# A three-operation kernel: converted weights stored from the source's tile, doubled conversion steps spread out, and a third of batch 0's factors loaded early into a tile of its own

## The chip, the cores and the metric

The kernel runs on one core of a Trainium2 chip. The metric is the device time of one execution in microseconds (us), as the median of several runs. The engines are named as in the profile: PE is TensorE (matmul), PEld its weight load, DVE is VectorE, ACT is ScalarE, POOL is GpSimd, and SP is the Sync engine, which here only issues transfers.

## The reference

Input `x` is 8 batches of 3072 positions by 256 channels. Three operations follow each other:

```python
X = np.fft.rfft(x, axis=1)
Yr = Xr @ w_r - Xi @ w_i + b_r ; Yi = Xr @ w_i + Xi @ w_r + b_i
Y  = sign(Y) * max(|Y| - 0.01, 0)          # on both parts
x  = irfft(Y, n=3072)                      # 24576 x 256 tokens
# soft mixture of 8 experts with 4 slots each
logits = x @ phi
d = softmax of logits over the tokens ; slots = d.T @ x
slots = relu(slots @ w1) @ w2              # per expert
c = softmax of logits over the 32 slots ; x = c @ slots
# feed-forward layer
h = x @ w_in                               # 256 -> 2048
out = (h * tanh(softplus(h))) @ w_out
```

`w_in` and `w_out` arrive as 64-bit floats, given to the kernel as pairs of 32-bit integers, so the kernel has to convert them to 32-bit floats itself.

## The kernel before, in words

The work falls into three stages. In the first, of about 610 us, the 8 batches are transformed, thresholded and transformed back, the logits and both softmaxes are formed, and the slots are summed up over all tokens. In the second, of about 25 us, the experts work on the 32 slots. In the third, of about 1210 us, the feed-forward layer runs over 48 blocks of 512 tokens, each in 8 steps, so 384 steps.

In the first stage the order of everything is written out by hand. `at(pos, fn, ...)` puts a piece of work at a position, the pieces are sorted by position and then issued one after the other, so each engine and each queue gets its own instructions in that order. The unit of the position is a step `k`: there are 4 steps to a batch, 32 in all, and each runs the linear part (`linear`, lines 306 to 331) for a quarter of the batch's frequencies. Around step `k` stand the second transform stage (`stage2`, lines 268 to 283), about one step ahead of the linear part that uses it, the loads of its input (`load_b`, line 255, tile `bt`, at k - 1.91, so for a step that comes later), the first stage of later batches (`load_x`, line 225, `stage1`, lines 238 and 241, `store_a`, line 248), and the softmax chain of the batch before (`sturn` to `ctrans`, lines 374 to 466), which repeats every four steps. `ctrans` writes the combination factors `c` of batch b to the DRAM tensor `c_d[b]`, once as rounded values and once as remainders; for batch 0 it does so at position 7.24.

In `linear` VectorE adds `p` (line 319), ScalarE makes `cl` and the other threshold from it (lines 326 and 327), and POOL subtracts the two into `yt` (line 328). `cl` has one buffer. All of these are in order on their engines with the conversions below.

The conversions (`conv`, lines 571 to 605) turn a piece of 128 x 256 weights into floats in seven small pieces of work: step 0 loads the integers into the tile `cvs` (line 578, on the Sync queue, two buffers); step 1 is a product on POOL into `cvc` (line 588, one buffer); steps 2 to 5 are four operations and a scaling on VectorE (lines 590 to 597) that use `cva`, `cvs` and `cvc`; step 6 is a sum on POOL (line 600 for `w_in`, line 604 for `w_out`). For `w_in` the sum is written over `cvc` and stored from there to the DRAM tensor `win_d`, by a transfer that POOL issues (line 601). For `w_out` the sum is written over the source's tile, and pieces of it are split later (`cut`, `sums`). There are 16 pieces of `w_in` and then 16 of `w_out`. Their places are the list `homes`: piece i has its VectorE work at `homes[i]`, its load 0.6 ahead of that and its first POOL operation 0.21 ahead. Every step from 4 to 29 has a piece at k - 0.13, and six steps, 5, 7, 8, 10, 11 and 13, have a second one at k - 0.7.

Between the stages the loads for the third are issued on the Sync queue: two expert weights `raw` (line 853), `win` (line 778, from `win_d`), and the weight pairs `wc` and `whl` of the eight steps (`load_w`, line 772), and among them the factors `ctt` of batch 0 from `c_d[0]`, in two halves of four transfers of 192 KB each (`c_fetch`, line 810), the first half right behind the first weight pair, the second behind the third.

The third stage (`ffn`) starts with `prep`, which multiplies the expert outputs with `win` (line 949), splits the result, spreads it (line 959) and copies it to `mst` (lines 964 and 966). Step p then makes two `h` matmuls from `mst` and `ctt` (line 974), ScalarE gates them (line 990) into `g` or `u`, both engines split the results (lines 996 to 1020), and some steps later `omm` multiplies them with the weights into `oa` to `od` (lines 1033 and 1044). A block reads 8 of the 24 columns of `ctt`: blocks 0 and 1 of a batch the first 8, blocks 2 and 3 the next 8, blocks 4 and 5 the last. The first twelve-matmul step of `omm` is placed behind the `h` of step 3.

Of the kernel before, what the change touches and what calls it, by code (L numbers as in the profile page):

```python
# [8 lines left out]
F32 = mybir.dt.float32  # L9
# [4 lines left out]
ALU = mybir.AluOpType  # L14
# [56 lines left out]
def body(ctx, tc, x, w_r, w_i, b_r, b_i, phi, w1, w2, w_in, w_out, cbig, ct, out, dbg=None, stop=False):  # L71
# [5 lines left out]
    def at(pos, fn, *a):  # L77
        items.append((round(pos, 4), len(items), fn, a))
# [4 lines left out]
    cb = keep.tile([128, 128 * 3 + 32], F32, name="cb")  # L83
    f1, f1t, ident, sel = cb[:, 0:128], cb[:, 128:256], cb[:, 256:384], cb[:, 384:416]
    sit = keep.tile([128, 2, NS], F32, name="sit")
    win_d = dram.tile([D, FF], F32, name="win_d")
    wn_d = dram.tile([4, 128, 2, 2 * D], F32, name="wn_d")
    wf_d = dram.tile([4, 128, 2, 7 * 128], F32, name="wf_d")
# [485 lines left out]
    def conv(srcd, dstd, i, step):  # L574
        n, v, p = CW, nc.vector, nc.gpsimd
        if step == 0:
            cv["n", i] = late[1].tile([128, n, 2], I32, tag="cs", bufs=2, name="cvs")
            nc.sync.dma_start(out=cv["n", i], in_=srcd[i])
            return
        if step == 1:  # L580
            src = cv["src"] = cv.pop(("n", i))
            cv.update(lo=src[:, :, 0].bitcast(U32), hi=src[:, :, 1])
            for t in "ac":
                cv[t] = late[1].tile([128, n], I32, tag="c" + t, name="cv" + t)
        lo, hi, a, c = (cv[t] for t in ("lo", "hi", "a", "c"))
        if step == 1:
            hf = hi.bitcast(F32)
            p.tensor_tensor(c.bitcast(F32), hf, hf, op=ALU.mult)
        elif step == 2:
            v.tensor_scalar(a, hi, 5, 2, op0=ALU.logical_shift_left, op1=ALU.logical_shift_right)  # L590
            v.scalar_tensor_tensor(a, hi, -0x40000000, a, op0=ALU.bitwise_and, op1=ALU.bitwise_or)
        elif step == 3:
            v.scalar_tensor_tensor(a.bitcast(F32), c.bitcast(F32), TINY2, a.bitcast(F32), op0=ALU.is_ge, op1=ALU.mult)
        elif step == 4:
            v.tensor_scalar(hi, a, -0x800000, None, op0=ALU.bitwise_and)
        elif step == 5:
            v.scalar_tensor_tensor(c.bitcast(F32), lo, 2.0 ** -52, hi.bitcast(F32), op0=ALU.mult, op1=ALU.mult)
        else:
            if dstd is not None:
                p.tensor_tensor(c.bitcast(F32), a.bitcast(F32), c.bitcast(F32), op=ALU.add)  # L600
                p.dma_start(out=dstd[i], in_=c.bitcast(F32))
                return
            o = cv["src"].rearrange("p n t -> p (n t)").bitcast(F32)
            p.tensor_tensor(o[:, 0:n].rearrange("p (e a c) -> p a e c", e=2, a=4), a.bitcast(F32).rearrange("p (a e c) -> p a e c", e=2, a=4),
                            c.bitcast(F32).rearrange("p (a e c) -> p a e c", e=2, a=4), op=ALU.add)
            cv["o", i] = o
# [38 lines left out]

    SIDE = {b: [4 * b + z for z in (-5.825, -4.825, -4.525, -3.825, -2.825, -2.525)] for b in range(3, NB - 1)}

    at(-9, setup)
    at(-5.5, fill, 22)
    at(-5.2, weights)  # L650
    for c in range(4):
# [49 lines left out]
    si, di = view(w_in, win_d)  # L701
    so, do = [w_out.bitcast(I32).rearrange("(q p t) c -> q t p c", q=4, t=4)[i // 4][i % 4].rearrange("p (f t) -> p f t", t=2) for i in range(16)], None
    ncv = len(si) + len(so)
    homes = sorted([k - 0.13 for k in range(4, 30)] + [k - 0.7 for k in (5, 7, 8, 10, 11, 13)])
    assert len(homes) == ncv
    for i in range(ncv):
        s_, d_, ii = (si, di, i) if i < len(si) else (so, do, i - len(si))
# [26 lines left out]
    with tc.manual_schedule():  # L734
        for _, _, fn, a in sorted(items, key=lambda v: v[:2]):
            fn(*a)
        if dbg is not None:
            nc.sync.dma_start(out=dbg["m_all"], in_=m_run[(NB + 1) % 2])
            nc.sync.dma_start(out=dbg["ds_all"], in_=d_acc)
            nc.sync.dma_start(out=dbg["s_all"], in_=s_acc)  # L740
            nc.sync.dma_start(out=dbg["c0"], in_=c_d[0])
            nc.sync.dma_start(out=dbg["wout"], in_=wout_d)
            nc.sync.dma_start(out=dbg["win"], in_=win_d)

        left.close()
        if stop:
            ex.close()
            ctx_r.close()
            return

        big = ctx.enter_context(tc.tile_pool(name="big", bufs=1))
        win = big.tile([128, 16, D], F32, name="win")
        sot = big.tile([128, 2, NS], F32, name="sot")
        rep = big.tile([128, 2, 4, NS], F32R, name="rep")
        mstp = ctx.enter_context(tc.tile_pool(name="mstp", bufs=1))
        hsp = ctx.enter_context(tc.tile_pool(name="hsp", bufs=1))
        ctp = [ctx.enter_context(tc.tile_pool(name="ctp0", bufs=1))]
        ct_t = {}
        ht = mstp.tile([128, 2, 8, 128], F32, tag="mst", name="ht")
        hs = [hsp.tile([128, FE], F32, name="hs"), big.tile([128, FE], F32, tag="wof", bufs=2, name="hs")]  # L760
        w_t = {}

        def load_w(p, pool=None):
            if p in FAST:
                t = big.tile([128, 2048], F32R, tag="whl", bufs=4, name="whl")[:, 0:1792]
                src = wf_d[p // 2].rearrange("p r f -> p (r f)")
                w_t[p] = t.rearrange("p (r k m) -> p r k m", r=2, k=7)
            else:
                t = (big if pool is None else pool).tile([128, 4 * D], F32R, tag="wof" if pool is None else "wc%d" % p, bufs=2 if pool is None else 1, name="wc")
                src = wn_d[p // 2].rearrange("p r f -> p (r f)")  # L770
                w_t[p] = t.rearrange("p (r i e m) -> p r i e m", r=2, i=2, e=2)
            nc.sync.dma_start(out=t.bitcast(F32), in_=src)

        def load_rest(ex):
            for i in range(2):
                ex.load(2, 6 + i, None, big.tile([128, 8, D], F32, tag="whl", bufs=4, name="raw"))
            for h in range(2):
                nc.sync.dma_start(out=win[:, 8 * h:8 * h + 8].rearrange("p t d -> p (t d)"), in_=win_d[128 * h:128 * h + 128])
            load_w(0)
            c_fetch(tc, ctp, ct_t, c_d, 0, (0, 2))  # L780
            load_w(1)
            for i in range(2):
                for r in range(2):
                    s2 = sel[:, None, :].to_broadcast([128, 2, NS])
                    if i == r:
                        nc.vector.tensor_copy(rep[:, i, 2 * r:2 * r + 2], s2)
                    else:
                        nc.vector.tensor_scalar(rep[:, i, 2 * r:2 * r + 2], s2, 0.0, None, op0=ALU.mult)

        ex.run(hs, ht, psum, sit, ident, sot, load_rest)  # L790
        load_w(2)
        c_fetch(tc, ctp, ct_t, c_d, 0, (2, 4))
        load_w(3)
        ex.close()
        ctx_r.close()
        pst.close()
        psh = ctx.enter_context(tc.tile_pool(name="psh", bufs=2, space=PSUM))
        pso = ctx.enter_context(tc.tile_pool(name="pso", bufs=2, space=PSUM))
        mst = mstp.tile([128, FF], F32R, tag="mst", name="mst")
        ctp.append(ctx.enter_context(tc.tile_pool(name="ctp1", bufs=1)))  # L800
        ffn(ctx, tc, NB, mst, w_t, win, c_d, out.rearrange("(b p n) d -> b p n d", b=NB, n=N2), ctp, ct_t, psh, pso, sot, rep, load_w)


def c_fetch(tc, ctp, ct_t, c_d, b, js=(0, 4)):

    if js[0] == 0:
        ct_t[b] = ctp[b % 2].tile([128, N2, 128], F32R, tag="ct", name="ctt")
    n = slice(6 * js[0], 6 * js[1])
    for r in range(4):
        tc.nc.sync.dma_start(out=ct_t[b][32 * r:32 * r + 32, n].bitcast(F32).rearrange("s (j i) t -> s j (i t)", i=6),  # L810
                             in_=c_d[b][r % 2][js[0]:js[1]].rearrange("j s i t -> s j (i t)"))
# [109 lines left out]
FAST = (1, 3, 5, 7)  # L921


def ffn(ctx, tc, NB, mst, w_t, win, c_d, out, ctp, ct_t, psh, pso, sot, rep, load_w):

    nc = tc.nc
    gp = ctx.enter_context(tc.tile_pool(name="gp", bufs=2))
# [5 lines left out]
    h_t, s_t, acc = {}, {}, {}  # L933
    for p in range(4, 8):
        load_w(p, pmp)
    zero = pmp.tile([128, 256], F32, name="zero")
    nc.gpsimd.memset(zero, 0.0)

# [29 lines left out]
    def hidden(p):  # L968
        blk, c = divmod(p, NPR)
        b, m = divmod(blk, NB4)  # L970
        h_t[p] = [psh.tile([128, 512], F32, tag="h", name="h") for _ in range(2)]
        for i in range(2):
            f = 2 * c + i
            nc.tensor.matmul(h_t[p][i].rearrange("p (n t) -> p n t", n=8), lhsT=mst[:, f * 128:f * 128 + 128],  # L974
                             rhs=ct_t[b][:, 8 * (m // 2):8 * (m // 2) + 8, 64 * (m % 2):64 * (m % 2) + 64], start=True, stop=True)

    def gate(p):
        h = h_t.pop(p)
# [145 lines left out]
```

## Time and profile before

| | us |
|---|---|
| median of 3 runs | 1854.81 |
| lowest and highest of them | 1852.15, 1858.98 |
| profiled execution, its own time | 1850.49 |
| its span, first to last instruction | 1848.1 |
| PE busy | 1803.0 |
| DVE busy | 1506.6 |
| ACT busy | 1380.0 |
| POOL busy | 264.8 |

A busy share over the whole span mixes three stages with different limits, so it only says which engine to look at. A row of the timeline gives the start of an instruction, how long it took, its engine, its line in the kernel, what it writes and reads, and in brackets how long the engine stood still ahead of it and what ended that. The granted clock is a share of TensorE's full speed; 0.50 is the lower of its two levels, 1.2 GHz.

### The profile page before, as it was taken

To read this page: it belongs to the slowest core of one execution; us is meant where nothing else is said; L and a number is where in the kernel's file an instruction comes from. 1 tells how busy PE (TensorE), PEld (TensorE's weight loads), DVE (VectorE), ACT (ScalarE), POOL (GpSimd) and SP (SyncE) were. 2 spreads that over 40 slices of the span, in tenths; PEclk is the share of its full clock that TensorE was granted. 3 is DMA by queue.
4 is the path that set the end of the run, shared out by engine and by line. 5 is a ranking of instruction groups with operands and counts; after the bars stand their busy time and mean duration, and the time that the engine had idled before them with its cause. 6 is when DMAs were issued, how large, how long until landed. Compare 5 with 4: busy or idle time off the path is not lost.

```text
span 1848.1 us, 32080 instructions
## 1 busy us (share of the span) xinstructions
PE 1803.0 (98%) x12438; PEld 1547.6 (84%) x12438; DVE 1506.6 (82%) x2158; ACT 1380.0 (75%) x2237; POOL 264.8 (14%) x342
## 2 busy tenths in 40 slices
PE   7999999999998899999999999999999999999998
PEld 5777778887887488888888888888888888888887
DVE  5366867666667489999999999999999999999997
ACT  4665767767765388888888888888888888888885
POOL 0233433544542000000000000000000000000000
PEclk8999999999999999999999999999999999999999
DMA  7776756666654930020020011002002002000001
GB/s 177 181 183 171 185 154 172 185 181 166 165 156 179 341 106 24 24 54 16 24 58 24 23 34 43 17 24 58 24 23 58 19 17 58 24 23 24 24 19 29
DMA packets 174663, 159.99 MB, mean 87 GB/s; under 512 B 111392, under 2 KB 143776, under 8 KB 172592
## 3 DMA queue, kind: packets, MB, share of 16 engines
q1 hardware_dynamic: 166848, 147.16, 30.2%
q0 software_dynamic: 2656, 7.90, 1.3%
q10 hardware_dynamic: 5008, 2.88, 0.7%
q8 instruction: 98, 1.61, 0.4%
q14 instruction: 53, 0.43, 0.1%
HBM read 96.55 MB, written 61.34 MB: 85 GB/s over the span
## 4 chain that ended last, share of the span: by engine, by line
PE 86%; DVE 4%; issue 3%; ACT 3%; DMA 3%; POOL 2%; SPq 0%; POOLq 0%; DVEq 0%; ACTq 0%
PE oa L1033 14%; PE ob L1033 14%; PE h L974 10%; PE l L306 8%; PE oa L1044 7%; PE oc L1044 7%; PE od L1044 7%; PE s L268 4%; PE ob L1044 4%; PE s L238 2%; PE tr L361 2%; PE pp L339 1%; POOL yt L328 1%; PE sps L529 1%; DMA ctt<-c_d 1%
## 5 line engine op out<-in xcount | busy, mean ns | idle before, releaser
L1018 DVE TENSOR_TENSOR sl<-u,sh 128x1792 fp32r<-128x1792 f32 x192 | 387.7, 2019 | 1.1 <-ACT sh L1013 1.1
L990 ACT ACTIVATE g<-h 128x512 f32<-128x512 f32 x384 | 208.8, 595 | 149.0 <-PE h L974 145.2
L1020 DVE TENSOR_TENSOR gl<-g,gh 128x1024 fp32r<-128x1024 f32 x191 | 231.7, 1213 | 83.6 <-ACT gh L1001 83.6
L974 PE MATMUL h<-ctt,mst 128*128 128x512 f32 x768 | 242.4, 397 | 4.6 <-DMA ctt<-c_d 3.1
L1033 PE MATMUL oa<-gh,wc 128*128 128x512 f32 x768 | 238.9, 392 | 0.0
L1033 PE MATMUL ob<-gh,wc 128*128 128x512 f32 x768 | 236.8, 390 | 0.0
L1013 ACT ACTIVATE sh<-u 128x1024 fp32r<-128x1024 f32 x192 | 201.4, 1049 | 45.3 <-DVE u L1008 45.3
L990 ACT ACTIVATE u<-h 128x512 f32<-128x512 f32 x384 | 207.6, 593 | 9.5 <-PE h L974 0.4
L1001 ACT ACTIVATE gh<-g 128x1024 fp32r<-128x1024 f32 x191 | 202.9, 1062 | 6.1
L984 POOL TENSOR_TENSOR sh<-zero 128x256 fp32r<-128x256 f32 x48 | 37.8, 788 | 1137.6 <-PE ob L1044 1137.5
L326 ACT ACTIVATE cl<-p,tup 128x384 f32<-128x384 f32 x124 | 76.3, 616 | 143.2 <-DVE p L319 90.2
L1033 PEld LDWEIGHTS oa<-gh,wc 128*128 128x128 f32 x768 | 144.7, 189 | 34.0
L1033 PEld LDWEIGHTS ob<-gh,wc 128*128 128x128 f32 x768 | 144.5, 188 | 30.1
L999 ACT ACTIVATE sh<-u 128x768 fp32r<-128x768 f32 x192 | 162.7, 847 | 9.0
L328 POOL TENSOR_TENSOR yt<-cl,p 128x384 f32<-128x384 f32 x124 | 126.4, 1019 | 261.0 <-ACT p L327 168.2
L974 PEld LDWEIGHTS h<-ctt,mst 128*128 128x128 f32 x768 | 132.8, 191 | 22.7 <-ACT g L990 3.6
L1006 DVE TENSOR_TENSOR u<-u 128x512 f32<-128x512 f32 x192 | 150.6, 784 | 0.0
L1033 PE MATMUL oa<-gl,wc 128*128 128x512 f32 x384 | 150.4, 392 | 0.0
L1033 PE MATMUL ob<-gl,wc 128*128 128x512 f32 x384 | 149.4, 389 | 0.0
L1044 PE MATMUL od<-sh,whl 128*128 128x256 f32 x720 | 147.7, 281 | 0.0
L1044 PE MATMUL oa<-sh,whl 128*128 128x256 f32 x768 | 146.1, 283 | 0.0
L1044 PE MATMUL oc<-sh,whl 128*128 128x256 f32 x720 | 140.5, 283 | 0.0
(236 smaller groups left out, 3948.9 us busy)
## 6 DMA issues: line engine op xcount, KB each, us to landing
out_dram<-ot SPq DMA_DIRECT2D x380, 64.0 KB, 1.8
xc<-in_x_dram SPq DMA_DIRECT2D x84, 256.0 KB, 4.7
sdr<-a SPq DMA_DIRECT2D x84, 256.0 KB, 4.1
bt<-sdr SPq DMA_DIRECT2D x84, 256.0 KB, 5.6
ctt<-c_d SPq DMA_DIRECT2D x28, 384.0 KB, 6.8
w1t<-in_moe_w_dram SPq DMA_DIRECT2D x6, 1024.0 KB, 6.9
c_d<-chl SPq DMA_DIRECT2D x14, 384.0 KB, 3.0
w2t<-in_moe_w_dram SPq DMA_DIRECT2D x5, 1024.0 KB, 11.1
```

What stands on the lines that cost most here:

```text
L306: nc.tensor.matmul(full[:, 0:48 * nq].rearrange("p (q f) -> p q f", f=48), lhsT=ww[:, h, es], rhs=spec(xx, h), start=n == 0, stop=n == 5)
L328: nc.gpsimd.tensor_sub(o, cl, p)
L974: nc.tensor.matmul(h_t[p][i].rearrange("p (n t) -> p n t", n=8), lhsT=mst[:, f * 128:f * 128 + 128], rhs=ct_t[b][:, 8 * (m // 2):8 * (m // ...
L990: nc.scalar.activation(out=v[i], in_=h[i], func=AF.Mish)
L999: nc.scalar.activation(out=gh[:, 0:3], in_=g[:, 1:4], func=AF.Copy)
L1001: nc.scalar.activation(out=gh, in_=g, func=AF.Copy)
L1006: nc.vector.tensor_sub(g[:, 4:6], g[:, 0:1].to_broadcast([128, 2, 256]), g[:, 1:3])
L1013: nc.scalar.activation(out=gh[:, 3:7], in_=g[:, 4:8], func=AF.Copy)
L1018: nc.vector.tensor_sub(gl, g[:, 1:8], gh[:, 0:7].bitcast(F32))
L1020: nc.vector.tensor_sub(gl, g, gh.bitcast(F32))
L1033: nc.tensor.matmul(ps, lhsT=w[:, r, i, e], rhs=x[:, i], start=c == 0 and i == 0 and n == 0, stop=p == NQ - 2 and i == 1 and n == 2)
L1044: nc.tensor.matmul(ps[:, half], lhsT=w[:, r, k], rhs=y[:, x], start=False, stop=c == FAST[-1] and n == 2 and ((t, half) in (("c", 1), ("d" ...
```

## The change

There are three edits. First, the sum of a converted piece of `w_in` is written over the source's tile `cvs`, as that of `w_out` is already, and stored to `win_d` from there. Second, the six steps with two conversions are 6, 8, 10, 12, 14 and 16 in place of 5, 7, 8, 10, 11 and 13. Third, a tile `c0` of its own holds the first 8 columns of batch 0's factors; it is loaded at position 12.05 of the first stage by eight transfers on the Sync queue, and blocks 0 and 1 read it. The two half loads of `ctt` for batch 0 between the stages go; one whole load of four transfers is issued in `ffn` behind the last weight load.

```diff
--- before.py
+++ after.py
@@ -83,6 +83,7 @@
     cb = keep.tile([128, 128 * 3 + 32], F32, name="cb")
     f1, f1t, ident, sel = cb[:, 0:128], cb[:, 128:256], cb[:, 256:384], cb[:, 384:416]
     sit = keep.tile([128, 2, NS], F32, name="sit")
+    c0 = keep.tile([128, 8, 128], F32R, name="c0")
     win_d = dram.tile([D, FF], F32, name="win_d")
     wn_d = dram.tile([4, 128, 2, 2 * D], F32, name="wn_d")
     wf_d = dram.tile([4, 128, 2, 7 * 128], F32, name="wf_d")
@@ -596,11 +597,11 @@
         elif step == 5:
             v.scalar_tensor_tensor(c.bitcast(F32), lo, 2.0 ** -52, hi.bitcast(F32), op0=ALU.mult, op1=ALU.mult)
         else:
+            o = cv["src"].rearrange("p n t -> p (n t)").bitcast(F32)
             if dstd is not None:
-                p.tensor_tensor(c.bitcast(F32), a.bitcast(F32), c.bitcast(F32), op=ALU.add)
-                p.dma_start(out=dstd[i], in_=c.bitcast(F32))
+                p.tensor_tensor(o[:, 0:n], a.bitcast(F32), c.bitcast(F32), op=ALU.add)
+                p.dma_start(out=dstd[i], in_=o[:, 0:n])
                 return
-            o = cv["src"].rearrange("p n t -> p (n t)").bitcast(F32)
             p.tensor_tensor(o[:, 0:n].rearrange("p (e a c) -> p a e c", e=2, a=4), a.bitcast(F32).rearrange("p (a e c) -> p a e c", e=2, a=4),
                             c.bitcast(F32).rearrange("p (a e c) -> p a e c", e=2, a=4), op=ALU.add)
             cv["o", i] = o
@@ -645,7 +646,14 @@
 
     SIDE = {b: [4 * b + z for z in (-5.825, -4.825, -4.525, -3.825, -2.825, -2.525)] for b in range(3, NB - 1)}
 
+    def load_c0():
+        for r in range(4):
+            for j, n in ((0, 6), (1, 2)):
+                nc.sync.dma_start(out=c0[32 * r:32 * r + 32, 6 * j:6 * j + n].bitcast(F32).rearrange("s i t -> s (i t)"),
+                                  in_=c_d[0][r % 2][j][:, 0:n].rearrange("s i t -> s (i t)"))
+
     at(-9, setup)
+    at(12.05, load_c0)
     at(-5.5, fill, 22)
     at(-5.2, weights)
     for c in range(4):
@@ -701,7 +709,7 @@
     si, di = view(w_in, win_d)
     so, do = [w_out.bitcast(I32).rearrange("(q p t) c -> q t p c", q=4, t=4)[i // 4][i % 4].rearrange("p (f t) -> p f t", t=2) for i in range(16)], None
     ncv = len(si) + len(so)
-    homes = sorted([k - 0.13 for k in range(4, 30)] + [k - 0.7 for k in (5, 7, 8, 10, 11, 13)])
+    homes = sorted([k - 0.13 for k in range(4, 30)] + [k - 0.7 for k in (6, 8, 10, 12, 14, 16)])
     assert len(homes) == ncv
     for i in range(ncv):
         s_, d_, ii = (si, di, i) if i < len(si) else (so, do, i - len(si))
@@ -777,7 +785,6 @@
             for h in range(2):
                 nc.sync.dma_start(out=win[:, 8 * h:8 * h + 8].rearrange("p t d -> p (t d)"), in_=win_d[128 * h:128 * h + 128])
             load_w(0)
-            c_fetch(tc, ctp, ct_t, c_d, 0, (0, 2))
             load_w(1)
             for i in range(2):
                 for r in range(2):
@@ -789,7 +796,6 @@
 
         ex.run(hs, ht, psum, sit, ident, sot, load_rest)
         load_w(2)
-        c_fetch(tc, ctp, ct_t, c_d, 0, (2, 4))
         load_w(3)
         ex.close()
         ctx_r.close()
@@ -798,7 +804,7 @@
         pso = ctx.enter_context(tc.tile_pool(name="pso", bufs=2, space=PSUM))
         mst = mstp.tile([128, FF], F32R, tag="mst", name="mst")
         ctp.append(ctx.enter_context(tc.tile_pool(name="ctp1", bufs=1)))
-        ffn(ctx, tc, NB, mst, w_t, win, c_d, out.rearrange("(b p n) d -> b p n d", b=NB, n=N2), ctp, ct_t, psh, pso, sot, rep, load_w)
+        ffn(ctx, tc, NB, mst, w_t, win, c0, c_d, out.rearrange("(b p n) d -> b p n d", b=NB, n=N2), ctp, ct_t, psh, pso, sot, rep, load_w)
 
 
 def c_fetch(tc, ctp, ct_t, c_d, b, js=(0, 4)):
@@ -921,7 +927,7 @@
 FAST = (1, 3, 5, 7)
 
 
-def ffn(ctx, tc, NB, mst, w_t, win, c_d, out, ctp, ct_t, psh, pso, sot, rep, load_w):
+def ffn(ctx, tc, NB, mst, w_t, win, c0, c_d, out, ctp, ct_t, psh, pso, sot, rep, load_w):
 
     nc = tc.nc
     gp = ctx.enter_context(tc.tile_pool(name="gp", bufs=2))
@@ -933,6 +939,7 @@
     h_t, s_t, acc = {}, {}, {}
     for p in range(4, 8):
         load_w(p, pmp)
+    c_fetch(tc, ctp, ct_t, c_d, 0)
     zero = pmp.tile([128, 256], F32, name="zero")
     nc.gpsimd.memset(zero, 0.0)
 
@@ -972,7 +979,7 @@
         for i in range(2):
             f = 2 * c + i
             nc.tensor.matmul(h_t[p][i].rearrange("p (n t) -> p n t", n=8), lhsT=mst[:, f * 128:f * 128 + 128],
-                             rhs=ct_t[b][:, 8 * (m // 2):8 * (m // 2) + 8, 64 * (m % 2):64 * (m % 2) + 64], start=True, stop=True)
+                             rhs=(c0 if blk < 2 else ct_t[b])[:, 8 * (m // 2):8 * (m // 2) + 8, 64 * (m % 2):64 * (m % 2) + 64], start=True, stop=True)
 
     def gate(p):
         h = h_t.pop(p)
```

## Rows read from the trace of the kernel before

**Rows 1.** The profile page, part 1: busy time of each engine over the whole span

```profile
PE 1803.0 (98%) x12438; PEld 1547.6 (84%) x12438; DVE 1506.6 (82%) x2158; ACT 1380.0 (75%) x2237; POOL 264.8 (14%) x342
```

**Rows 2.** Busy time by stretch (us, busy and instructions per engine, clock, DMA share, GB/s)

```profile
123.60:127.00 3.40, 3.40 (x11) 2.80 (x10) 3.17 (x7) 2.17 (x7) 1.05 (x2) 0.50 0.72 169
...
164.50:168.00 3.50, 3.50 (x23) 1.07 (x25) 1.82 (x6) 1.84 (x4) 0.79 (x2) 0.51 0.12 42
...
639.00:649.25 10.25, 8.24 (x16) 5.08 (x17) 6.54 (x9) 7.80 (x12) 0.00 (x0) 0.50 1.03 308
...
100.00:280.00 180.00, 170.41 (x1438) 136.68 (x1437) 125.88 (x261) 114.80 (x245) 69.57 (x91) 0.98 0.66 169
...
300.00:480.00 180.00, 178.86 (x1639) 147.56 (x1628) 121.22 (x258) 127.07 (x276) 78.53 (x101) 1.00 0.66 178
```

**Rows 3.** Timeline of TensorE, 100 to 280 us: start, us, engine, line, [idle before <-releaser]

```profile
122.53 0.45 PE L306 MATMUL l<-xh,ah 128*128 128x384 f32 x1 [1.95 <-ACT a L241]
...
163.35 0.42 PE L306 MATMUL l<-xh,bh 128*128 128x384 f32 x1 [2.99 <-DVE xl L283]
...
186.06 0.65 PE L238 MATMUL s<-xc,f 64*64 64x512 f32 x2 [0.95 <-DVE xl L281]
...
212.93 0.48 PE L474 MATMUL dps<-dx,cb 128*128 128x256 f32 x1 [0.37 <-ACT dx L427]
...
238.41 0.42 PE L306 MATMUL l<-xh,bh 128*128 128x384 f32 x1 [1.60 <-DVE xl L283]
...
274.86 0.59 PE L383 MATMUL lps<-v,cb 128*128 128x384 f32 x1 [1.70 <-DVE xl L281]
```

**Rows 4.** Waits of all engines, 100 to 280 us: total us, times, longest us

```profile
ACT cl L326 <- DVE p L319: 37.0, 21, 4.7
...
POOL cvc L588 <- DMA win_d<-cvc: 31.5, 9, 7.0
...
DVE cva L593 <- POOL cvc L588: 14.0, 7, 4.5
```

**Rows 5.** Timeline of one doubled conversion, 105 to 116 us, in order of time

```profile
105.12 0.63 POOL L601 DMA_DIRECT2D win_d<-cvc  x1 [0.30 <-POOL cvc L600]
...
112.74 0.61 POOL L588 TENSOR_TENSOR cvc<-cvs 128x256 f32<-128x256 f32 x1 [6.99 <-DMA win_d<-cvc]
...
113.38 1.23 DVE L593 SCALAR_TENSOR_TENSOR cva<-cvc,cva 128x256 f32<-128x256 f32 x1 [4.54 <-POOL cvc L588]
...
115.96 0.61 ACT L326 ACTIVATE cl<-p,tup 128x384 f32<-128x384 f32 x1 [4.66 <-DVE p L319]
```

**Rows 6.** Tile k: one pair in each of 32 steps (ns; first and last start us)

```profile
L310 ACT ACTIVATE k<-l x64: 469/493/552, 43.2 to 582.8; 128x384 f32<-128x384 f32 x64
```

**Rows 7.** Tile cvc: time of its stores to win_d, from issue to landing

```profile
DMA to landing us min/median/max: 2.2/3.4/7.5
```

**Rows 8.** Line 255 at 104 to 106 us (ns min/median/max; landing), and its first reader

```profile
L255 SPq DMA_DIRECT2D bt<-sdr x3: 448/449/601, 104.3 to 105.4; - x3
...
DMA to landing us min/median/max: 7.0/7.4/7.9
...
116.39 1.86 PE L268 MATMUL s<-tall,bt 96*128 96x144 f32 x13
```

**Rows 9.** Timeline and tile ctt at the opening of the last stage, 622 to 640 us

```profile
L810 SPq DMA_DIRECT2D ctt<-c_d x4: 303/432/477, 622.5 to 624.5; - x4
...
633.83 0.16 PEld L949 LDWEIGHTS oc<-win,sot 128*32 128x32 f32 x8 [0.96 <-DMA win<-win_d]
...
636.93 1.29 DVE L966 CAST mst<-oa 128x512 fp32r<-128x512 f32 x2 [0.59 <-PE oa L959]
...
639.98 1.19 PE L974 MATMUL h<-ctt,mst 128*128 128x512 f32 x2 [3.08 <-DMA ctt<-c_d]
```

**Rows 10.** Chain that ended last: twelve-matmul steps (start, us, what), first and second

```profile
646.04 2.56 PE oa L1033 x6
...
655.46 1.37 PE oa L1033 x6
```

## The prediction, made before the changed kernel was run

> **What bounds the kernel now.** I read the page first: TensorE is busy for 98% of the span, so time can come only from stretches in which it stands still or runs slowly [rows 1]. The busy time by stretch shows where. From 100 to 280 us TensorE is busy 170.4 of 180 us, so it idles 9.6 us; from 300 to 480 us, where the same loop runs without doubled conversions and without stores of converted `w_in`, it idles 1.1 us. In the earlier stretch there are also two pieces of 3.4 and 3.5 us at a granted clock of 0.50 and 0.51, the lower level (1.2 of 2.4 GHz) [rows 2].
>
> The timeline of TensorE then gives the idle time piece by piece: 1.95, 2.99, 0.95, 0.37, 1.60 and 1.70 us, together 9.6 [rows 3]. There are six, as there are doubled steps (5, 7, 8, 10, 11, 13), and in that order they belong to each other. The two low pieces of the clock begin right behind the longest two, at 123.6 and 164.5 us.
>
> What ends them is seen in the list of waits: POOL's first operation of a conversion (line 588) waits 31.5 us in nine times for the store of the conversion before, VectorE 14.0 us for POOL, ScalarE 37.0 us for VectorE [rows 4]. One case in order of time: the store is issued at 105.12; POOL can write `cvc` again only at 112.74, after 6.99 us; VectorE, whose line 593 is queued ahead of the next `p`, stands for 4.54 us, ScalarE for 4.66; TensorE, further ahead, for 1.95 us at 122.53 [rows 3, 5]. The reason is in the code: `cvc` has one buffer and the store reads it.
>
> The second place is the opening of the last stage. The weights `mst` are ready at 636.93 + 1.29 = 638.2 us, but the first matmul starts at 639.98, released by a landing of `ctt` [rows 9]. Until 649.25 the clock is 0.50 [rows 2].
>
> **The sum.** I make it against the profiled execution, 1850.5 us with a span of 1848.1; the shown median is 1854.8, 4.3 us higher, and I take the same saving from that.
>
> Store from the source's tile. Instructions and bytes stay: 16 sums on POOL and 16 stores, written to the other tile. What goes is POOL's wait. What comes is a wait on the Sync queue: the load of conversion i+2 goes into the tile that the store of i still reads. In the code the tightest case lies 0.40 of a step behind the store, once in each doubled step; a step is (582.8 - 43.2) / 31 = 17.4 us [rows 6], so that is 7.0 us. Such a store lands after 2.2 to 7.5 us, median 3.4 [rows 7]. With the median the new wait is nothing, with the worst about 0.5 us; behind the load on that queue stand `sdr` stores and `xc` loads, then the `bt` loads of the next steps, and the `bt` load that I found tight lands at 105.4 + 7.9 = 113.3 for a reader at 116.39, so 3.1 us of cover [rows 8]. I cost it at 0; without the cover it is the rival below.
>
> The Trainium skill ("DMA: Bandwidth & Descriptors", the section on the anatomy of one DMA by the gpsimd path) puts such a transfer at 2.0 us plus bytes over 436 GB/s, an estimate of 2.3 us for 128 KB, and warns that completion of a write to HBM can take surprisingly long. The rows differ from its figure, with 3.4 and up to 7.5 us, and the measurement decides; by 2.3 us the new wait would never show. Its warning speaks against the change, since the wait for completion is moved to another engine and not removed.
>
> Steps two apart. The six doubled steps become 6, 8, 10, 12, 14 and 16. The softmax chain of a batch repeats every four steps, so 6, 10 and 14 stand where 10 stood, and 8, 12 and 16 where 8 stood. Those two had the small stalls, 0.37 and 0.95 us [rows 3]. Even with no help from the store, what is left is 3 x 0.37 + 3 x 0.95 = 4.0 us, a gain of 5.6. At best nothing is left, a gain of 9.6; at worst the second conversion still stalls as now, a gain of 0. I take 5.6, nearest to rows of the same places. What is late next there is VectorE's `xl`, the releaser of four of the six.
>
> The clock. The two low pieces are full of matmuls, so at the full level they would take half: 1.7 us each, 3.4 together. Both follow an idle time of 1.95 us or more, while none follows the stalls of 0.95, 1.60 and 1.70 (the two alone make the mean of 0.98 over 180 us) [rows 2, 3]. The two stalls go, so I take 3.4; the ends are 0 and 3.4.
>
> Factors in a tile of their own. Eight loads of `ctt` (192 KB) leave the crowded opening, four of 384 KB go behind the weights, and eight small ones (512 KB in all) come at position 12.05. The first matmul then waits for `mst`, ready 1.7 us earlier. The ends are 0, if something else is late, and 2.7: the prep matmuls wait 0.96 us for `win`, and with 0.77 MB less in its way that may go too [rows 9]. I take 1.7. The four late loads are first read by block 2: 384 steps fill (1848.1 - 640) us, 3.15 each, so 16 steps give 50 us of cover. The new loads at 12.05 cost the Sync queue 8 x 0.43 = 3.5 us by the issue time of their like [rows 9], ahead of a `bt` load with some 3.1 us to spare at the tightest [rows 8]; cost 0 to 1 us, I take 0, as that one is the tightest.
>
> Sum: 5.6 + 3.4 + 1.7 = 10.7 us. 1850.5 - 10.7 = 1839.8 for the profiled execution, 1854.8 - 10.7 = **1844.1** for the median, which is 0.58%. What measurement of this kernel can tell from no change is about 0.5%, 9.3 us.
>
> **The rivals.** (a) VectorE, not the store, bounds a doubled step. Four of the six stalls end with its `xl`, and it is busy 125.9 of 180 us [rows 2, 3]; two conversions in one step stay two. Then the stalls and the low clock stay, moved to other steps, and only the opening gains: 1854.8 - 1.7 = 1853.1. Against it: from 300 to 480 us it is busy 121.2 us, nearly as much, with 1.1 us of TensorE idle.
>
> (b) The opening keeps the full clock. After the change TensorE idles about 1.4 us ahead of the first matmul, less than 1.70, after which no drop came [rows 3]. The first twelve-matmul step on `oa` took 2.56 us against 1.37 in the second [rows 10], so 1.2 us lie in `oa` alone; TensorE is busy 8.2 us in that piece of low clock [rows 2], so 4.1 is the most. I take 3.0, as the four pairs of `h` and `ob` lie in it too: 1841.1. Against it: TensorE works little from 635 us on in any case.
>
> (c) Slower: the Sync queue. Where a store lands 7.5 us late to a load that waits on it at once, as when POOL lags, `bt` behind it slips by 7.5 - 3.1 = 4.4 us beyond its cover [rows 7, 8]. In five doubled steps with `w_in` that is 22 us, and 1844.1 + 22 = 1866. It decides as soon as the slip is over 2.1 us in each of the five (10.7 / 5). Against it: 7 us of distance by position, and POOL lags less once its own wait is gone.
>
> The change does what it says by the code; no wait for the store is left on POOL, since `cvc` is then read by POOL alone at the end.
>
> **How the numbers follow.** The forecast has 0.52, (a) 0.28, (b) 0.12, (c) 0.08. The forecast's own range goes from a gain of 7.9 (half of the 5.6 lost) to 9.6 + 3.4 + 2.7 = 15.7: 1839 to 1847. The range, 1837 to 1853.5, adds (b) with its spread and (a), and leaves out (c) and the edges. Faster by over 0.5% are (b) and some three quarters of the forecast, as (15.7 - 9.3) of its 7.8 us lie there: 0.39 + 0.12 = 0.51. Within 0.5% are the other quarter and (a): 0.41. Slower is (c): 0.08.
>
> **What would show it.** Right: no row of POOL's line 588 waiting for a store; TensorE idle below 5 us from 100 to 280; no low clock there; the first `h` released by ScalarE or VectorE near `mst`'s end. Wrong: stalls of 1.5 us or more ended by `xl` around steps 6, 8, 12, 14; Sync waits for `win_d` stores of several us with TensorE waiting for `bt`; the first `h` still released by a DMA.

## The result, and the profile after

The changed kernel took 1838.05 us in the median of four runs (1836.15 to 1840.91), the kernel before 1854.4 (1852.15 to 1858.98): ratio 0.991 with a 95% interval of 0.9887 to 0.9933. That is 16.4 us less, and 12.4 to 21.0 by the interval. The profiled executions stand at 1836.15 and 1850.49 us, 14.3 apart, and their spans at 1833.9 and 1848.1, 14.2 apart. The forecast was 1844.1 with a range of 1837.0 to 1853.5: right in direction and inside the range, but 6 us too cautious.

The runs that follow were made in three sets on three chips, each with the kernel before beside it, so a time is compared only with the time before of its own set (medians of 1853.55, 1855.49 and 1851.4).

TensorE's busy time in the page falls by 4.3 us of 1803.0, so most of the 14.2 us is time in which it stood still:

```profile
PE 1798.7 (98%) x12438; PEld 1545.7 (84%) x12438; DVE 1504.6 (82%) x2158; ACT 1379.2 (75%) x2237; POOL 265.9 (14%) x342
```

The windows of [rows 2], in the changed kernel (busy us of PE, PEld, DVE, ACT, POOL; clock; DMA share; GB/s):

```profile
100.00:280.00 180.00, 177.99 (x1525) 145.00 (x1524) 132.61 (x278) 123.37 (x262) 72.05 (x92) 1.00 0.71 185
...
300.00:480.00 180.00, 178.46 (x1572) 145.43 (x1567) 119.92 (x255) 128.63 (x281) 82.89 (x111) 1.00 0.67 180
...
628.40:635.20 6.80, 6.06 (x13) 4.28 (x14) 5.81 (x9) 6.25 (x10) 0.00 (x0) 0.50 1.04 388
```

From 100 to 280 us TensorE now idles 180 - 177.99 = 2.0 us in place of 9.6, and the mean clock there is 1.00 in place of 0.98: both low pieces are gone. The third row is the low piece of the opening; it is 6.8 us long, where it was 10.2.

What TensorE still waits for from 100 to 280 us, by the list of its waits (us in total, times, longest), are six pieces of at most 0.5 us, and VectorE's `xl` is not among them:

```profile
PE dps L475 <- ACT dx L428: 1.0, 3, 0.4
...
PE mb L420 <- DVE mdg L403: 0.7, 2, 0.5
...
PE mt L399 <- ACT y L367: 0.3, 1, 0.3
```

In the list of all engines' waits for the same stretch POOL's first operation of a conversion (line 589 now) waits for a load once, and for no store. The wait for stores stands in the Sync queue's list (whole span), as forecast, but it is small:

```profile
POOL cvc L589 <- DMA cvs<-in_moe_w_in_dram: 1.4, 1, 1.4
```

```profile
SPq L579 <- DMA win_d<-cvs: 2.0, 4, 0.9
```

To see how far a stage has moved, I take tile `k`, which ScalarE writes first in each step, from the first write of step 4 to the first of step 31 (the last two numbers of a row, us). Before and after:

```profile
L310 ACT ACTIVATE k<-l x55: 469/493/552, 105.7 to 581.2; 128x384 f32<-128x384 f32 x55
```

```profile
L311 ACT ACTIVATE k<-l x55: 469/493/552, 105.7 to 570.0; 128x384 f32<-128x384 f32 x55
```

That is 475.5 us before and 464.3 after, 11.2 less; up to step 4 nothing differs (105.7 in both). The busy times of that stretch, before and after, say what went:

```profile
105.67:581.23 475.56, 461.89 (x4066) 380.24 (x4065) 331.07 (x697) 321.25 (x687) 201.80 (x263) 0.99 0.62 164
```

```profile
105.70:570.02 464.32, 458.40 (x4066) 378.60 (x4065) 328.81 (x697) 320.69 (x687) 202.71 (x263) 1.00 0.64 170
```

The number of matmuls, 4066, is the same. TensorE idles 5.9 us in place of 13.7, so 7.8 less, and is busy for 3.5 us less, which is what the two low pieces of the clock had cost. The rest of the 14.2 us comes at the opening. In the timeline of the changed kernel there:

```profile
625.46 1.29 DVE L973 CAST mst<-oa 128x512 fp32r<-128x512 f32 x2 [0.59 <-PE ob L966]
...
626.20 0.74 PE L981 MATMUL h<-c,mst 128*128 128x512 f32 x2 [0.77 <-DVE mst L973]
```

The first `h` starts 0.74 us behind the start of the first copy to `mst`; before it was 639.98 - 636.93 = 3.05 us [rows 9]. From there to the end, by the rows of the tiles `mst` and `h` (first and last start), it is 1814.1 - 625.5 = 1188.6 us to the last `h`, where the kernel before took 1828.2 - 636.9 = 1191.3. Before, then after:

```profile
L966 DVE CAST mst<-oa x2: 681/686/692, 636.9 to 637.5; 128x512 fp32r<-128x512 f32 x2
...
L974 PE MATMUL h<-ctt,mst x768: 388/396/796, 640.0 to 1828.2; 128*128 128x512 f32 x192
```

```profile
L973 DVE CAST mst<-oa x2: 681/686/692, 625.5 to 626.1; 128x512 fp32r<-128x512 f32 x2
...
L981 PE MATMUL h<-ctt,mst x736: 389/392/400, 671.7 to 1814.1; 128*128 128x512 f32 x184
```

So 11.2 + 2.7 us, and 0.3 between step 31 and `mst`, make the 14.2.

### The profile page after: what moved, and what is told of

Its sections match the earlier page's. It is cut to its first block, busy times and chain, and to the rows that moved or that the text cites. A ratio compares the mean times of both kernels' runs of the same rounds, so it can differ in the third digit from the quotient of the medians.

```text
span 1833.9 us, 32086 instructions
## 1 busy us (share of the span) xinstructions
PE 1798.7 (98%) x12438; PEld 1545.7 (84%) x12438; DVE 1504.6 (82%) x2158; ACT 1379.2 (75%) x2237; POOL 265.9 (14%) x342
## 4 chain that ended last, share of the span: by engine, by line
PE 91%; DVE 3%; ACT 2%; DMA 2%; issue 1%; POOL 1%; SPq 0%; DVEq 0%; ACTq 0%; POOLq 0%
PE oa L1040 14%; PE ob L1040 14%; PE h L981 10%; PE l L307 9%; PE oa L1051 8%; PE oc L1051 7%; PE od L1051 7%; PE s L269 6%; PE ob L1051 4%; PE s L239 2%; PE tr L362 2%; PE pp L340 2%; PE sps L530 1%; DMA wst<-in_w_r_dram 1%; PE iu L351 1%
## 5 line engine op out<-in xcount | busy, mean ns | idle before, releaser
L981 PE MATMUL h<-ctt,mst 128*128 128x512 f32 x736 | 229.5, 393 | 0.0
L320 DVE TENSOR_TENSOR p<-l,k 128x384 f32<-128x384 f32 x128 | 69.3, 550 | 87.9 <-PE l L307 38.5
```

## The experiments

Two theories stood after this result. S: POOL's wait for the store is the cause, so taking it away does the work. P: the places of the doubled steps are the cause, as the prediction's sum had it. The first four runs take the edits apart. Lines are numbered 588 or 589, and so on, by whether the third edit is in.

**The first edit alone.**

```diff
+            o = cv["src"].rearrange("p n t -> p (n t)").bitcast(F32)
             if dstd is not None:
-                p.tensor_tensor(c.bitcast(F32), a.bitcast(F32), c.bitcast(F32), op=ALU.add)
-                p.dma_start(out=dstd[i], in_=c.bitcast(F32))
+                p.tensor_tensor(o[:, 0:n], a.bitcast(F32), c.bitcast(F32), op=ALU.add)
+                p.dma_start(out=dstd[i], in_=o[:, 0:n])
                 return
-            o = cv["src"].rearrange("p n t -> p (n t)").bitcast(F32)
```

> The kernel before with the first edit alone: the sum of a piece of w_in is written over the source's tile and stored from there; the doubled steps stay 5, 7, 8, 10, 11, 13. Theory S (POOL's wait for the store is the cause of the stalls): no wait of POOL for a store of win_d, TensorE idle from 100 to 280 us falls from 9.6 to between 2 and 4 us, no low clock in there, span 1848.1 -> 1838 to 1840. Theory P (the places of the doubled steps are the cause, VectorE is full there): the stalls ended by VectorE's xl stay, idle 7 to 9 us, low clock stays, span 1845 or more.

1839.45 us against 1853.55 before, ratio 0.9917 (0.9902 to 0.9932). Tile `k` as above, then TensorE's waits and the busy times from 100 to 280 us, and the busy times from step 4 to step 31:

```profile
L310 ACT ACTIVATE k<-l x55: 469/493/557, 105.3 to 567.0; 128x384 f32<-128x384 f32 x55
```

```profile
PE l L306 <- DVE xl L283: 0.6, 1, 0.6
...
PE dps L474 <- ACT dx L427: 0.3, 1, 0.3
```

```profile
100.00:280.00 180.00, 179.16 (x1536) 146.96 (x1534) 136.96 (x286) 125.07 (x266) 76.17 (x97) 1.00 0.72 185
...
105.28:567.02 461.74, 457.35 (x4066) 378.82 (x4065) 329.60 (x697) 320.84 (x687) 203.28 (x263) 1.00 0.64 169
```

461.7 us, 13.8 less than before, with 0.9 us of waits and the doubled steps at their old places. The stalls of 1.60 to 2.99 us at steps 5, 7, 11 and 13 are gone though the conversions stand where they stood. This speaks for S, and it is more than the changed kernel's 11.2: TensorE idles 4.4 us from step 4 to step 31, 9.3 less than before, and is busy for 4.5 us less. S itself was too cautious: it had 2 to 4 us of idle left, and a span of 1838 to 1840 where the profile has 1833.7.

**The second edit alone.**

```diff
-    homes = sorted([k - 0.13 for k in range(4, 30)] + [k - 0.7 for k in (5, 7, 8, 10, 11, 13)])
+    homes = sorted([k - 0.13 for k in range(4, 30)] + [k - 0.7 for k in (6, 8, 10, 12, 14, 16)])
```

> The kernel before with the second edit alone: doubled steps 6, 8, 10, 12, 14, 16, the store still from cvc. Theory S: POOL still waits some 30 us in about nine times, idle from 100 to 280 us between 5 and 9 us, span 1841 to 1846. Theory P, and the sum of the prediction, which took the gain from the places alone: idle about 4.0 us, no low clock, span about 1839.

1843.08 us against 1853.55, ratio 0.9942 (0.9926 to 0.9959). Tile `k`; then two rows of the list of waits from 100 to 280 us; then two of TensorE's stalls, at steps 8 and 10:

```profile
L310 ACT ACTIVATE k<-l x55: 469/493/552, 107.1 to 572.3; 128x384 f32<-128x384 f32 x55
```

```profile
POOL cvc L588 <- DMA win_d<-cvc: 16.5, 8, 3.2
...
DVE cva L593 <- POOL cvc L588: 2.9, 2, 1.6
```

```profile
179.59 0.65 PE L238 MATMUL s<-xc,f 64*64 64x512 f32 x2 [0.83 <-DVE xl L281]
...
206.34 0.48 PE L474 MATMUL dps<-dx,cb 128*128 128x256 f32 x1 [0.36 <-ACT dx L427]
```

465.2 us, 10.3 less than before. POOL still waits 16.5 us for stores, half of the 31.5 [rows 4], but TensorE hardly notices: its waits from 100 to 330 us, which take in step 16, sum to 3.1 us, where the prediction's 3 x 0.37 + 3 x 0.95 gave 4.0 for the six steps. At steps 8 and 10 they are 0.83 and 0.36. The forecast of S, some 30 us of POOL's wait and 5 to 9 us of idle, failed; that of P, about 4.0, was near. But the run does not part the place from the wait, since the edit shortens the wait too: the longest is 3.2 us in place of 7.0, and it reaches VectorE's line 593 for 2.9 us in place of 14.0 [rows 4]. So the second edit breaks the same chain further along, and each of the two edits removes most of the same stalls; they do not add.

**The third edit alone.** The factors' tile, its load at 12.05 and the moved load of `ctt`, as in the diff above; the two other edits undone.

> The kernel before with the third edit alone (the factors' tile). Both theories: the steps of the first stage run as before up to 600 us with 9.6 us of idle; the first h starts 0.7 us behind the start of the first copy to mst (before 3.05), not 1.7 us earlier as predicted but 2.3 to 2.6 earlier; span 1848.1 -> 1845 to 1845.5.

1849.73 us in the median of ten runs against 1853.55, ratio 0.9982 (0.997 to 0.9993). Tile `k`; TensorE's waits from 100 to 280 us; a low piece of the clock that was not there before; tiles `mst` and `h`:

```profile
L311 ACT ACTIVATE k<-l x55: 470/493/552, 108.6 to 586.6; 128x384 f32<-128x384 f32 x55
```

```profile
PE l L307 <- DVE xl L284: 4.7, 2, 2.5
```

```profile
241.30:244.70 3.40, 3.40 (x16) 1.35 (x18) 2.53 (x7) 1.75 (x5) 0.58 (x1) 0.51 0.11 39
```

```profile
L973 DVE CAST mst<-oa x2: 680/686/692, 642.1 to 642.7; 128x512 fp32r<-128x512 f32 x2
...
L981 PE MATMUL h<-ctt,mst x736: 389/392/400, 688.1 to 1830.4; 128*128 128x512 f32 x184
```

The opening gains as expected: 1830.4 - 642.1 = 1188.3 us, 3.0 less than before. But the first stage did not stay: 478.0 us, 2.5 more, with a third low piece at 241.3 us behind a stall at step 11 that has grown from 1.60 to 2.19, and the stall at step 13 has grown from 1.70 to 2.86. Both theories missed that. POOL's line 589 at these two places, in the timeline:

```profile
236.57 0.61 POOL L589 TENSOR_TENSOR cvc<-cvs 128x256 f32<-128x256 f32 x1 [4.52 <-DMA win_d<-cvc]
...
276.02 0.61 POOL L589 TENSOR_TENSOR cvc<-cvs 128x256 f32<-128x256 f32 x1 [4.56 <-DMA win_d<-cvc]
```

It waits 4.52 and 4.56 us for the store, where it waited 3.74 and 1.43 before: the two stores took 6.1 and 6.5 us to land, before 5.4 and 3.3. The new load, issued from 258.2 to 262.5, comes only after step 11's stall and is over at step 13's. So I put the 2.5 us down to stores that happened to land later and not to the edit; that is argued from one execution and not shown. The ten runs speak for it: this profile is of a run of 1852.43 us, 2.7 above their median, and the gain by the medians, 3.8 us (1.3 to 5.6 by the interval), agrees with the 3.0 of the opening.

**The first two edits without the third.**

> The first and second edit without the third. Both theories: the first stage as in the changed kernel (idle 2.0 us from 100 to 280), the opening as before with the first h released by ctt; span 1836.5 to 1837.5, so 3 us above the changed kernel. If parts interact through the Sync queue (the load of the new tile stands ahead of a bt load), the first stage is shorter than in the changed kernel by up to 1 us.

1838.51 us, ratio 0.9917 (0.9902 to 0.9932) against 1853.55.

```profile
L310 ACT ACTIVATE k<-l x55: 470/493/553, 107.0 to 571.1; 128x384 f32<-128x384 f32 x55
```

464.1 us, the changed kernel's 464.3: the new load at 12.05 costs the first stage nothing that can be seen. So the first and second edit together are 2.4 us longer in this stretch than the first alone.

The next runs ask what it is in the first edit that gains, and whether the place matters once the wait is gone.

**Two buffers for `cvc`,** and nothing else changed in the kernel before:

```diff
-                cv[t] = late[1].tile([128, n], I32, tag="c" + t, name="cv" + t)
+                cv[t] = late[1].tile([128, n], I32, tag="c" + t, bufs=2 if t == "c" else 1, name="cv" + t)
```

> The kernel before, with two buffers for cvc and nothing else: the store reads one while the next conversion writes the other, doubled steps 5, 7, 8, 10, 11, 13 as before, no new wait on the Sync queue. Theory S (what the first edit gains is POOL's wait for the store and nothing else): from step 4 to step 31 some 462 to 464 us, as with the first edit alone (461.7; before 475.6), TensorE idle under 2 us from 100 to 280. Rival Q (the first edit gains by what else it moves: the tile that is written, the Sync queue held back by its new wait): 468 us or more.

One run, 1840.02 us, against 1855.49 before.

```profile
L310 ACT ACTIVATE k<-l x55: 466/493/557, 107.4 to 569.5; 128x384 f32<-128x384 f32 x55
```

```profile
PE l L306 <- DVE xl L283: 0.6, 1, 0.6
...
PE dps L474 <- ACT dx L427: 0.3, 1, 0.3
```

462.1 us, and the same two short waits as with the first edit alone. Q falls: neither the other tile nor the Sync queue does it. What gains is that POOL need not wait for a store. It is one run, but the 13.4 us of this stretch are far outside the 0.6 us by which the changed kernel's two profiles differ in it (464.3, and 463.7 below).

**The changed kernel with the doubled steps at odd places,** 5, 7, 9, 11, 13, 15:

> The changed kernel with the doubled steps at 5, 7, 9, 11, 13, 15: still two apart, but at the places of the softmax chain where the kernel before had its long stalls (5, 7, 11, 13). Theory S: with the store's wait gone the place hardly matters, from step 4 to step 31 462 to 466 us (changed kernel 464.3), idle under 3 us. Theory P: stalls of 1.5 us and more ended by xl come back at 5, 7, 11, 13 and with them a low clock, 470 us or more.

One run, 1837.18 us, against 1855.49 before.

```profile
L311 ACT ACTIVATE k<-l x55: 467/493/553, 107.4 to 570.5; 128x384 f32<-128x384 f32 x55
```

463.1 us, with no stall above 0.6 us from 100 to 280: with the wait gone, the busy places are as good as the others. P falls as a cause by itself; the places matter only while the wait is there.

**The opening filled with matmuls.** The changed kernel with 11 matmuls more, whose result is not read:

```diff
+        busy = bank("d", 1)
+
+        def fill(n):
+            for _ in range(n):
+                nc.tensor.matmul(busy, lhsT=c0[:, 0], rhs=c0[:, 0:4].rearrange("p n t -> p (n t)"), start=True, stop=True)
+
+        fill(3)
         hl = pmp.tile([128, 2, 512], F32R, name="hl")
...
+        fill(3)
+        return fill
...
-    prep()
+    fill = prep()
...
             hidden(p)
+            if p < 3:
+                fill((2, 1, 2)[p])
             gate(p)
```

> The changed kernel with 11 matmuls more that read the factors' tile and whose result nobody reads, put into the gaps of TensorE at the opening of the last stage (3 behind the win product, 3 behind the spreading, 2, 1 and 2 behind the first three pairs of h). If the opening's low clock (6.8 us) comes from TensorE working little there, it stays at full clock and the last h comes up to 2 us earlier against the first copy to mst; if the extra matmuls only delay the pairs of h, the stage is 0 to 2 us longer.

1835.73 us, ratio 0.9898 (0.9882 to 0.9915) against 1855.49. The window of 10 us from 626 us, in the changed kernel and in this one, and then this one's rows of `mst` and `h`:

```profile
626.00:636.00 10.00, 8.59 (x21) 5.56 (x21) 8.32 (x13) 8.39 (x14) 0.00 (x0) 0.66 1.02 375
```

```profile
626.00:636.00 10.00, 9.30 (x34) 5.43 (x34) 7.82 (x11) 9.07 (x15) 0.00 (x0) 1.00 1.03 411
```

```profile
L980 DVE CAST mst<-oa x2: 681/686/692, 626.5 to 627.1; 128x512 fp32r<-128x512 f32 x2
...
L990 PE MATMUL h<-ctt,mst x736: 389/392/400, 671.0 to 1813.3; 128*128 128x512 f32 x184
```

The clock is 1.00 in place of 0.66, and from the first copy to the last `h` it is 1813.3 - 626.5 = 1186.8 us, 1.8 less than the changed kernel. So the low clock was what the opening still paid, and with the 11 matmuls in TensorE's gaps it does not come. The same stretch in the other profiles bears this out: without the third edit it is 1190.8 to 1192.0 us (five profiles, low piece 10.2 us or more), with it 1188.3 to 1189.0 (five, low piece 6.8 us each), and with the fill 1186.8 (two, no low piece).

**The first and third edit,** the doubled steps left at 5, 7, 8, 10, 11 and 13:

> The first and third edit without the second: the doubled steps stay 5, 7, 8, 10, 11, 13. Theory S, with what the four single parts gave (first edit alone 461.7 us from step 4 to 31, first and second 464.1): 461.5 to 462.5 us, span 1830 to 1832, time 1833 to 1836, a little faster than the changed kernel. If the load of the new tile at 12.05 collides with the doubled step 13, as it seemed to with the third edit alone (stall of 2.86 us at step 13 in place of 1.70): 463 us or more, and no faster than the changed kernel.

1836.62 us, ratio 0.9903 (0.9888 to 0.9918) against 1855.49.

```profile
L311 ACT ACTIVATE k<-l x55: 467/493/552, 107.4 to 569.9; 128x384 f32<-128x384 f32 x55
```

462.5 us, as with the first edit alone, and no collision at step 13. In span the gain over the changed kernel did not show: it is 1833.8, above the 1830 to 1832 expected, since step 4 began at 107.4 us in this profile and at 105.7 in the changed kernel's. That beginning has come between 105.1 and 108.6 us in the twelve profiles. It is no effect of the edits, since already the first row of `k` comes at 43.0 to 46.7 us, ahead of the load for the first conversion (88 us or later). How much of the spread of one kernel's runs it makes up is not shown.

**The best of it, beside the changed kernel.** First and third edit, old places, and the fill, then the changed kernel again on the same chip:

> First and third edit, doubled steps at their old places 5, 7, 8, 10, 11, 13, and the 11 matmuls that fill the opening. If the parts add: from step 4 to 31 462.5 us (changed kernel 464.3), from the first copy to mst to the last h 1186.8 us (changed kernel 1188.6), together 3.6 us less than the changed kernel at the same beginning. If the beginning (the start of step 4 has come between 105.3 and 108.6 us in the runs) outweighs it, the times of the two overlap.

> The changed kernel itself, beside the one above on the same chip. Theory S: 464.3 us from step 4 to 31 and 1188.6 us from the first copy to mst to the last h, as in its first profile; what differs from that profile is the beginning up to step 4, 105.3 to 108.6 us, which no part of the change touches. Its median some 2 to 4 us above the kernel above.

1832.91 us (1831.66 to 1835.88; ratio 0.9898, 0.9883 to 0.9913, against 1851.4 before) and 1838.12 us (1836.22 to 1838.91; ratio 0.9923, 0.9909 to 0.9936). The two do not overlap, and the medians are 5.2 apart, more than the 2 to 4 expected. Tile `k` of the one and of the other:

```profile
L311 ACT ACTIVATE k<-l x55: 467/493/557, 105.1 to 567.3; 128x384 f32<-128x384 f32 x55
```

```profile
L311 ACT ACTIVATE k<-l x55: 467/493/560, 106.6 to 570.3; 128x384 f32<-128x384 f32 x55
```

462.2 us, and 463.7, where the same kernel's first profile had 464.3. From the first copy to the last `h` it is 1186.8 and 1188.4 us. So the two stretches give 1.5 + 1.6 = 3.1 us, near the 3.6 expected, and the beginning, 105.1 against 106.6, another 1.5 that is no merit of the kernel. The four profiles with the wait gone and even places lie from 463.7 to 464.3 us, the four with old places from 461.7 to 462.5. So once the wait is gone the second edit costs some 1.9 us of the first stage. Why it does is not shown; against the first edit alone TensorE idles 1.5 us more in the changed kernel (5.9 and 4.4).

## Why the prediction was right, and where it was off

**The chain of causes was right.** Store, POOL's `cvc`, VectorE's line 593, ScalarE, TensorE [rows 4, 5]: two buffers for `cvc` take away the first link alone and the stalls go, but for 0.9 us.

**The stalls: 5.6 forecast, 7.6 measured** (9.6 to 2.0). I took the lower value from the places alone and gave the first edit nothing on its own. As the price of the places it was good: with the second edit alone TensorE waits 3.1 us to step 16, against 4.0 forecast. But the step "Even with no help from the store" put the gain on the wrong edit. The store's edit by itself is worth 13.8 us of the first stage, the places by themselves 10.3, both 11.2 to 11.8, since they remove the same stalls. The first edit alone went beyond the bound of 9.6 + 3.4 = 13.0 that I had for the two terms: 9.3 us of idle time and 4.5 of busy time, of which the two low pieces explain 3.4. Where the other 1.1 come from is open.

**The clock: 3.4 forecast, 3.5 measured,** as the difference of TensorE's busy time over the same matmuls; the two low pieces are gone, with both edits and with either alone. The two terms together, 9.0 forecast, gave 11.2.

**The opening: 1.7 forecast, 2.7 measured.** I let the first `h` wait for both copies of VectorE to `mst`, 1.29 us; it waits for the first alone. So `ctt` had cost 3.05 - 0.74 = 2.3 us. The other 0.4 lie behind the first `h`; the low piece of the clock is 3.4 us shorter there, which I had not counted, but that it gave the 0.4 is not shown. The 0.3 us ahead of `mst` agree with the wait for `win`, 0.96 us before and 0.4 after; but with the first edit alone, where `ctt` still stands between, it was 0.5, so the third edit is not shown to be the reason.

**The new wait: 0 forecast,** 2.0 us on the Sync queue in four times, the longest 0.9 where I had 0.5 at worst, and nobody behind it was late: no load stands among TensorE's waits. The estimate of 2.3 us from the Trainium skill ("DMA: Bandwidth & Descriptors", Anatomy of one DMA — SWDGE (gpsimd) path) was about the least that such a store took, and not the usual time: 2.2 to 7.5 us, median 3.4 [rows 7]. Its warning that completion can take long agrees with the 7.5 us, though no run here shows how much of them is completion. The wait was moved to a queue that could bear it.

**The load at 12.05: 0 forecast.** Its issue took 4.7 us, not 3.5, and left the `bt` load behind it about 1.5 us ahead of its reader in the changed kernel; with and without it the first stage is the same (464.3, 464.1). It was free, but closer than I had it.

**The rivals.** (a) fell: VectorE does two conversions in one step at the old places, with 0.9 us of waits. There it is busy 137.0 of 180 us where it was busy 125.9, as the same work is done in less time, so it was no bound. (b) did not come; a low piece of 6.8 us stayed though TensorE's waits ahead of it were under 0.8 us. So my reason, that no drop came behind a stall of 1.70 us or less, fell. The length of one stall does not tell in any case: with the third edit alone a drop began behind 1.71 us and none behind 2.86. The price of (b) was 3.0, the fill shows 1.8. (c) did not come.

**The range, and some luck.** By the medians the saving was 16.4 us, by the profiles 14.3, and with both kernels run again on another chip 13.3. The 2 us between the first two can't be told from the spread of the runs (1836.15 to 1840.91). The forecast's own range ended at 15.7, or 1839; the median of 1838.05 lies below it, and inside the whole range only by the room left for (b), which did not come. The sum came near because the first and the second edit each remove most of the stalls alone, not because I had priced the right one.

## What to carry to other kernels

When an engine that works in order for others also stores a result, let the store read a tile that the engine does not need again soon: a second buffer of 1 KB a partition was worth about as much here as moving the store to another tile (13.4 and 13.8 us of the first stage). Before costing two remedies of one stall, ask which of them would do alone, since they do not add and the second can cost. And where a stage opens with waits on every side, look at the granted clock there: matmuls that nobody reads can pay for themselves, as 11 did here with 1.8 us.

## What was not expected of the hardware

VectorE's line 593 (128x256, two inputs in SBUF) has two lengths, some 0.42 us, and mostly 1.03 us or more (one of 0.87). In the kernel before 21 of 32 are long, and each of them overlaps a `yt` of POOL, as at 113.38 [rows 5], where POOL's `yt` runs from 113.32 for 1.00 us; of the 11 short ones four do. This agrees with the Trainium skill ("SBUF — State Buffer", Who interferes with whom), by which a VectorE instruction with two SBUF inputs contends with a GpSimd instruction that reads SBUF. In the changed kernel the median is short, with the first edit alone it is long (ns, least, median, most):

```profile
L594 DVE SCALAR_TENSOR_TENSOR cva<-cvc,cva x32: 424/426/1212, 102.1 to 535.7; 128x256 f32<-128x256 f32 x32
```

```profile
L593 DVE SCALAR_TENSOR_TENSOR cva<-cvc,cva x32: 424/1036/1253, 101.7 to 532.9; 128x256 f32<-128x256 f32 x32
```

And yet the second kernel's first stage is the shorter one by 2.6 us. So I do not read anything of the gain into these lengths.
